# One decode step of grouped-query attention with a cached context and a dense ReLU layer: the closing products on one group of columns, and wo loaded in other pieces

## The chip, the cores and the metric

The kernel runs on one core of one Trainium2 chip. All arithmetic is in 32-bit floats. The time is the device time of one execution in microseconds (us), the median of several runs. Beside the runs there is one profiled execution, with a record of every instruction on TensorE (PE for products, PEld for the loads of their weights), VectorE (DVE), ScalarE (ACT), GpSimd (POOL), of the DMA queues, and of the clock that TensorE was granted.

## The reference

One token x of 512 values is normalized. Its attention goes over 65536 cached keys and values, 32 query heads sharing 8 key and value heads; beside it runs a layer with 1792 hidden values; both results are added to x.

```python
x = A_x
xn = _layernorm(x, axis=-1)
return x + _A_ref(xn, A_k_cache, A_v_cache, A_wq, A_wo) + _B_ref(xn, B_w1, B_w2)

# _A_ref: D = 512, Hq, Hkv, Sk, Dh = 32, 8, 65536, 128
q = (x @ wq).reshape(B, Sq, Hq, Dh).transpose(0, 2, 1, 3)
scores = jnp.einsum("bhqd,bhkd->bhqk", q, k) * (Dh ** -0.5)
o = jnp.einsum("bhqk,bhkd->bhqd", _softmax(scores, axis=-1), v)
return o.transpose(0, 2, 1, 3).reshape(B, Sq, Hq * Dh) @ wo
# _B_ref: Dff = 1792
return jnp.einsum("bsf,fd->bsd", jnp.maximum(jnp.einsum("bsd,df->bsf", x, w1), 0), w2)
```

## The kernel before, in words

Two large buffers in the on-chip memory hold what is streamed in: `ks` for keys, later for w1 and w2, and `vs` for wq, then for values, later for wo. All large loads are issued by SyncE (SP) on one queue, in program order.

**Start.** x is normalized and q = xn @ wq is made from 32 slices of wq (line 279).

**Attention.** 8 heads with 4 steps each, 32 steps in all. A step multiplies one load of keys with the queries (line 343), takes the maximum and the exponentials, and multiplies the values with the weights so made (line 359, accumulated in `acc_o`). SP refills `ks` or `vs` as soon as the step that read it lets go of it.

**End.** After the last keys SP loads w1 and w2 into `ks`, and after the last values wo into `vs`, as 32 slices of 512 columns (`load_slices`, which issues one DMA for each entry of `WO` and keeps a mark for each slice: the semaphore of the DMA that brings it). PE then works in this order:

1. h = relu(xn @ w1): 16 products (line 442), then the heads' results are put together and divided (lines 452 to 493). The outcome is `hT`, the weights for the products with w2, and `sw`, those for the products with wo.
2. Four small products that add x to `acc_y` (line 513).
3. 14 products with w2 (`FB` = 14), written by `gather`, line 504. Each multiplies a column of 128 weights with a slice of 128 x 512 and adds the row of 512 that comes out to `acc_z`. In the records each such product is two weight loads and two matmul instructions.
4. 28 products with the first slices of wo (`DIRECT` = 28), the same `gather`.
5. DVE copies `acc_z` to `rows` (line 535) as soon as slice 27 is done.
6. Slices 28 and 29 of wo go straight to `acc_y` as four products of 128 columns each (line 539). Then come four products that sum `rows` over its 128 partitions into `acc_y` (line 524), and slices 30 and 31.
7. DVE transposes `acc_y` to `yt` (line 551), and SP writes y out.

The kernel addresses TensorE's columns of weights in four groups: a product whose output starts at row 0, 32, 64 or 96 of the accumulator stands on column group 0, 1, 2 or 3. `gather(c, ...)` writes row 32c of `acc_z` and so stands on group c; the calls give it `j % CT` with `CT` = 4, so that the products take the four groups by turns. The rows of `acc_z` that no product writes were set to zero at the start; the sum over all partitions in step 6 adds up whichever rows were used.

Between the products nothing sets the order but the order of the program and the marks: the first w2 product waits for `hT` and for w2, the first wo product for `sw` and its piece of wo, and a later one for its own piece.

Of the kernel before, what the change touches and what calls it, by code (L numbers as in the profile page):

```python
# [16 lines left out]
D = 512  # L17
# [4 lines left out]
CT = 4  # L22
# [12 lines left out]
R = HKV  # L35
SLICES = R * G
WQ = [4, 28]
WO = [16, 8, 4, 2, 1, 1]
DIRECT = 28
EPS = 1e-5  # L40

# [27 lines left out]
def attention_and_mlp_kernel(  # L69
# [32 lines left out]
    def place(name, *shape, rows=P):  # L102
        return nc.alloc_sbuf_tensor(name, [rows, *shape], F32).ap()
# [36 lines left out]
    total, oT, hT = place("total", HQ), place("oT", HQ), place("hT", 4 * CT)  # L140
# [11 lines left out]
    def load(engine, name, dst, src, n=16):  # L152
        sem = nc.alloc_semaphore(name)
        engine.dma_start(dst, src).then_inc(sem, n)
        return sem, n


    def load_slices(name, src, counts):
        marks = []
        for n in counts:  # L160
            cut = slice(len(marks) * D, (len(marks) + n) * D)
            marks += [load(sy, f"{name}{len(marks)}", vs[:, cut], src[:, cut])] * n
        return marks
# [152 lines left out]
    t1, t2 = ks[:, : A * DFF], ks[:, A * DFF : A * DFF + FB * D]  # L316
    w1_in = load(sy, "w1_in", t1, w1.rearrange("p a f -> p (a f)"))
    w2_in = load(sy, "w2_in", t2, w2.rearrange("p j n -> p (j n)"))
    sy.wait_ge(v_free, 1)
    wo_in = load_slices("wo", wo.rearrange("h (i r) g f -> (h i) (r g f)", r=R), WO)  # L320

# [47 lines left out]
    with nc.Fori(0, HKV, engines=[ENG.DVE], head_slot={ENG.DVE: 110}):  # L369
# [36 lines left out]
        last = bias[:, NP - 1, :G].unsqueeze(1).to_broadcast([P, NP - 1, G])  # L406
# [56 lines left out]
    for j in range(2):  # L463
# [4 lines left out]
    hT_in = DV.op(lambda e: e.tensor_copy(hT.rearrange("p (c j) -> p c j", c=CT), hid), hid_in)  # L468
# [23 lines left out]
    sw_in = DV.op(  # L492
        lambda e: e.reduce_sum(
            sw.rearrange("p (r g) -> p r g", r=R), spread.rearrange("p r h g -> p r g h"), axis=AX.X
        ),
        DV.mark,
    )
# [3 lines left out]
    def gather(c, lhsT, row, marks, last=False):  # L501

        PE.op(
            lambda e: e.matmul(acc_z[32 * c : 32 * c + 1, :], lhsT, row, start=c not in begun, stop=last),  # L504
            *marks,
        )
        begun.add(c)
# [6 lines left out]
            x4_in,  # L514
        )
    for j in range(FB):
        gather(j % CT, hT[:, j : j + 1], t2[:, j * D : (j + 1) * D], [hT_in, w2_in])

    for j in range(SLICES):
        if j == SLICES - 2:  # L520

            for c in range(CT):
                PE.op(
                    lambda e: e.matmul(  # L524
                        acc_y[32 * c : 32 * c + 1, :P], ones[:, 0:1], rows[:, c * P : (c + 1) * P],
                        start=False, stop=False,
                    ),
                    folded,
                )
        row = vs[:, j * D : (j + 1) * D]  # L530
        lhsT = sw[:, j : j + 1]
        if j < DIRECT:
            gather(j % CT, lhsT, row, [sw_in, wo_in[j]], last=(j >= DIRECT - CT))
            if j == DIRECT - 1:
                folded = DV.op(lambda e: e.tensor_copy(rows, acc_z), PE.mark)  # L535
        else:
            for c in range(CT):
                PE.op(
                    lambda e: e.matmul(  # L539
                        acc_y[32 * c : 32 * c + 1, :P], lhsT, row[:, c * P : (c + 1) * P],  # L540
                        start=False, stop=(j == SLICES - 1),
                    ),
                    sw_in, wo_in[j],
                )
# [47 lines left out]
```

## Time and profile before

| | |
|---|---|
| time, median of 3 runs | 1303.25 us (1303.14 to 1303.85) |
| span of the profiled execution | 1303.1 us |
| PE busy with products | 666.8 us (51%) |
| PE loading weights | 187.1 us (14%) |
| DVE / ACT / POOL busy | 268.4 / 76.0 / 4.1 us |
| DMA queue of SP, share of 16 engines | 99.6% |
| read from the memory outside the core | 560.99 MB, 431 GB/s over the span |

The span runs from the first to the last instruction of the profiled execution; it lies 0.15 us under the median of the runs. Busy time of an engine is the union of its instructions. A row of the timeline gives the start, the length, the engine, the line, the output and the inputs, the shape, and how many instructions were merged into the row; in brackets stands how long the engine was idle before it and what ended that.

### The profile page before, as it was taken

The page shows a single profiled execution, that of the slowest core. Times are in us where ns is not written, and L with a number is a line of the kernel's source. Part 1 is how long each engine was busy: PE and PEld are TensorE (multiplying, and loading weights), DVE is VectorE, ACT ScalarE, POOL GpSimd, SP SyncE. Part 2 cuts the span into 40 slices and gives each one's busy share as a digit, 9 for nine tenths or more (in the row PEclk, how much of TensorE's full clock was granted, in tenths as well). Part 3 has the DMA queues.
Part 4 walks back from the last instruction along what each step waited for, and adds up shares of the span by engine and source line. Part 5 has one row for each costly group of instructions (what it writes and reads, how often), then busy time and mean ns, then how long its engine had stood idle before and what let it go on. Part 6 is the DMA issues. An engine that isn't in the chain of part 4 may idle for free. (4 is left out here: it accounts for less than half of the span.)

```text
span 1303.1 us, 10664 instructions
## 1 busy us (share of the span) xinstructions
PE 666.8 (51%) x4512; PEld 187.1 (14%) x4512; DVE 268.4 (21%) x398; ACT 76.0 (6%) x292; POOL 4.1 (0%) x22
## 2 busy tenths in 40 slices
PE   3355456455446545545545545544544644553657
PEld 1111111111111111111111111111111111111111
DVE  2221122221112222012222112222112222211222
ACT  0000000000000000000000000000000000000000
POOL 0000000000000000000000000000000000000000
PEclk9676676777677677667677677767767766767768
DMA  9999999999999999999999999999999999999998
GB/s 419 419 418 449 420 449 420 449 420 449 420 449 420 449 420 435 435 422 445 420 449 420 449 420 449 420 449 420 449 420 439 431 422 445 420 449 420 449 418 359
DMA packets 10957, 561.06 MB, mean 431 GB/s; under 512 B 1476, under 2 KB 1480, under 8 KB 1864
## 3 DMA queue, kind: packets, MB, share of 16 engines
q1 hardware_dynamic: 10800, 561.00, 99.6%
q8 instruction: 3, 0.05, 0.0%
q10 hardware_dynamic: 152, 0.00, 0.0%
q14 instruction: 2, 0.02, 0.0%
HBM read 560.99 MB, written 0.00 MB: 431 GB/s over the span
## 5 line engine op out<-in xcount | busy, mean ns | idle before, releaser
L359 PE MATMUL acc_o<-vs,wt 128*16 128x512 f32 x2048 | 298.5, 748 | 176.0 <-PEq L355 176.0
L343 PE MATMUL pa<-ks,qcur 128*32 128x512 f32 x1024 | 177.1, 824 | 321.6 <-PEq L338 321.6
L375 DVE STREAM_TRANSPOSE tr<-pa 128x1024 f32<-128x1024 f32 x64 | 80.0, 1250 | 411.1 <-PE pa L343 411.1
L343 PE MATMUL pb<-ks,qcur 128*32 128x512 f32 x1024 | 141.6, 673 | 0.0
L421 ACT ACTIVATE wt<-tr,bias 128x128 f32<-128x128 f32 x128 | 64.3, 511 | 1085.3 <-ACTq L419 1085.3
L359 PEld LDWEIGHTS acc_o<-vs,wt 128*16 128x16 f32 x2048 | 70.0, 114 | 377.7 <-issue 377.7
L343 PEld LDWEIGHTS pa<-ks,qcur 128*32 128x32 f32 x1024 | 39.0, 134 | 429.7 <-issue 421.7
L375 DVE STREAM_TRANSPOSE tr<-pb 128x1024 f32<-128x1024 f32 x64 | 80.0, 1250 | 51.5 <-PE pb L343 51.5
L401 DVE SCALAR_TENSOR_TENSOR acc<-acc,alpha,acc_o 128x512 f32<-128x512 f32 x24 | 18.0, 748 | 352.2 <-PE acc_o L359 352.2
L343 PEld LDWEIGHTS pb<-ks,qcur 128*32 128x32 f32 x1024 | 42.5, 133 | 108.8 <-issue 89.7
L348 PE MATMUL pm<-ident,m 128*4 128x128 f32 x32 | 10.4, 326 | 87.7 <-DVE m L387 67.2
L399 DVE COPY acc<-acc_o 128x512 f32<-128x512 f32 x8 | 5.5, 691 | 121.5 <-PE acc_o L359 121.5
L349 PE MATMUL pm<-dg,ones 4*128 4x4 f32 x64 | 15.8, 315 | 21.4 <-DVE dg L391 21.4
L384 DVE TENSOR_REDUCE mc<-tr 128x4 f32<-128x512 f32 x24 | 24.1, 1006 | 1.8
L421 ACT ACTIVATION_READ_ACCUMULATOR wt<-tr,bias 128x1 f32 x128 | 23.9, 187 | 0.0
L348 PEld LDWEIGHTS pm<-ident,m 128*4 128x4 f32 x32 | 2.6, 81 | 116.8 <-DVE m L387 89.0
L349 PEld LDWEIGHTS pm<-dg,ones 4*128 4x128 f32 x64 | 13.0, 252 | 29.2 <-DVE dg L391 29.2
L350 PE MATMUL pm<-dg,rowg 4*128 4x1 f32 x64 | 15.1, 302 | 0.0
L279 PE MATMUL pa<-vs,tr 128*8 128x512 f32 x64 | 9.9, 772 | 8.6 <-DMA vs<-wq 7.3
L350 PEld LDWEIGHTS pm<-dg,rowg 4*128 4x128 f32 x64 | 13.9, 266 | 0.0
L504 PE MATMUL acc_z<-vs,sw 128*1 128x512 f32 x56 | 9.1, 817 | 6.2 <-DMA vs<-wo 6.2
L389 DVE TENSOR_REDUCE mg<-pm 4x1 f32<-4x128 f32 x32 | 8.9, 279 | 13.4 <-PE pm L348 13.4
(98 smaller groups left out, 94.6 us busy)
## 6 DMA issues: line engine op xcount, KB each, us to landing
vs<-wq SPq DMA_DIRECT2D x1, 7168.0 KB, 21.2
ks<-w SPq DMA_DIRECT2D x2, 3584.0 KB, 22.5
vs<-wo SPq DMA_DIRECT2D x1, 4096.0 KB, 16.9
vs<-wo SPq DMA_DIRECT2D x1, 2048.0 KB, 21.5
vs<-wq SPq DMA_DIRECT2D x1, 1024.0 KB, 4.6
vs<-wo SPq DMA_DIRECT2D x1, 1024.0 KB, 23.5
ks<-k SPq DMA_DIRECT2D x32, 28.8
vs<-v SPq DMA_DIRECT2D x32, 28.9
```

What stands on the lines that cost most here:

```text
L279: lambda e: e.matmul(pr[32 * c : 32 * c + HKV, :], xs[:, i, :], vs[:, i * 512 : (i + 1) * 512], start=(i < CT), stop=(i >= SLICES - CT),),
L343: i = te.matmul(tile_of[32 * c : 32 * c + 32, :], qcur, ks[:, at : at + TW], start=True, stop=True)
L348: te.transpose(pm[:G, :P], m, ident)._wait_ge(s_dve, 3).then_inc(s_max, 1)
L349: te.matmul(pm[:, P : P + G], ones[:G, :], dg[:, :G], start=True, stop=True)._wait_ge(s_dve, 4)
L350: te.matmul(pm[:, P + G : P + G + 1], rowg, dg[:, G : G + 1], start=True, stop=True).then_inc(s_max, 1)
L359: mm = te.matmul(acc_o[32 * c : 32 * c + WIDE * G, :], wt[:, i * WIDE : (i + 1) * WIDE, :].rearrange("p b g -> p (b g)"), vs[:, i * 512 : ...
L375: i = ve.transpose(tr[:, s * SUB : (s + 2) * SUB, :].rearrange("p b i -> p (b i)"), (pa, pb)[s // 2 % 2].rearrange("p i k -> p (i k)"),)._ ...
L384: i = ve.reduce_max(top, tr[:, :, :G].rearrange("p b g -> p g b"), axis=AX.X)
L389: ve.reduce_max(mg, pm[:G, :P], axis=AX.X)._wait_ge(s_max, 1)
L401: ve.scalar_tensor_tensor(flat, flat, alpha[:, n : n + 1], acc_o, op0=ALU.mult, op1=ALU.add)
L421: i = se.activation(wt[:, :, g], tr[:, :, g], AF.Exp, bias=bias[:, n, g : g + 1], scale=scale, accum_out=part[:, n, g : g + 1],)
L504: lambda e: e.matmul(acc_z[32 * c : 32 * c + 1, :], lhsT, row, start=c not in begun, stop=last),
```

## The change

The products with w2 and those with the first 24 slices of wo all stand on column group 0. Slices 24 to 27 of wo go on by turns over the four groups. wo comes in seven DMAs of 8, 8, 8, 4, 2, 1 and 1 slices; it was six, of 16, 8, 4, 2, 1 and 1.

```diff
-WO = [16, 8, 4, 2, 1, 1]
+WO = [8, 8, 8, 4, 2, 1, 1]
+SINGLE = 24
 DIRECT = 28
...
     for j in range(FB):
-        gather(j % CT, hT[:, j : j + 1], t2[:, j * D : (j + 1) * D], [hT_in, w2_in])
+        gather(0, hT[:, j : j + 1], t2[:, j * D : (j + 1) * D], [hT_in, w2_in])
...
         if j < DIRECT:
-            gather(j % CT, lhsT, row, [sw_in, wo_in[j]], last=(j >= DIRECT - CT))
+            gather(0 if j < SINGLE else j % CT, lhsT, row, [sw_in, wo_in[j]], last=(j >= DIRECT - CT))
```

On SP the loads at the program's end stood as follows before (`ks<-w` is w1 and w2; a slice of wo has 512 columns, so 128x8192 is a piece of 16 slices):

```order
L154 DMA ks<-w 128x7168 [waits k_free]
L154 DMA ks<-w 128x7168
L154 DMA vs<-wo 128x8192 [waits v_free]
L154 DMA vs<-wo 128x4096
L154 DMA vs<-wo 128x2048
L154 DMA vs<-wo 128x1024
L154 DMA vs<-wo 128x512 x2
```

And with the change:

```order
L155 DMA ks<-w 128x7168 [waits k_free]
L155 DMA ks<-w 128x7168
L155 DMA vs<-wo 128x4096 [waits v_free]
L155 DMA vs<-wo 128x4096 x2
L155 DMA vs<-wo 128x2048
L155 DMA vs<-wo 128x1024
L155 DMA vs<-wo 128x512 x2
```

The piece of 16 became two pieces of 8; everything else on SP keeps its place.

On PE the products and their order stay the same, 14 with w2 and 28 with wo. Their waits before, from the first w2 product on (`wo16` is the semaphore of the piece that begins with slice 16; the semaphore of the first row is one of the framework's that was used again, and carries w2's landing):

```order
L504 MATMUL acc_z<-ks,hT 1x512 [waits Activation_sequencer_49]
L504 MATMUL acc_z<-ks,hT 1x512 x13
L504 MATMUL acc_z<-vs,sw 1x512 [waits wo0,dve]
L504 MATMUL acc_z<-vs,sw 1x512 x15
L504 MATMUL acc_z<-vs,sw 1x512 [waits wo16]
L504 MATMUL acc_z<-vs,sw 1x512 x7
L504 MATMUL acc_z<-vs,sw 1x512 [waits wo24]
L504 MATMUL acc_z<-vs,sw 1x512 x3
L539 MATMUL acc_y<-vs,sw 1x128 [waits wo28]
```

And with the change:

```order
L505 MATMUL acc_z<-ks,hT 1x512 [waits Activation_sequencer_49]
L505 MATMUL acc_z<-ks,hT 1x512 x13
L505 MATMUL acc_z<-vs,sw 1x512 [waits wo0,dve]
L505 MATMUL acc_z<-vs,sw 1x512 x7
L505 MATMUL acc_z<-vs,sw 1x512 [waits wo8]
L505 MATMUL acc_z<-vs,sw 1x512 x7
L505 MATMUL acc_z<-vs,sw 1x512 [waits wo16]
L505 MATMUL acc_z<-vs,sw 1x512 x7
L505 MATMUL acc_z<-vs,sw 1x512 [waits wo24]
L505 MATMUL acc_z<-vs,sw 1x512 x3
L540 MATMUL acc_y<-vs,sw 1x128 [waits wo28]
```

One wait is new, before slice 8. The rows don't show the column group; it is in the address of the output alone.

## The prediction

> **What bounds the kernel now.** I read the page's table of slices first, then the chain that ended last, then the timeline of the last 25 us.
>
> ```profile
> PE   3355456455446545545545545544544644553657
> DMA  9999999999999999999999999999999999999998
> DMA vs<-wo 1%; PE acc_o L359 1%; PE acc_z L504 1%; DVE rows L535 0%; PE acc_y L539 0%; DVE yt L551 0%; PE acc_y L524 0%; DVEq L397 0%
> ```
>
> The DMA engines are busy in every slice while PE is busy half the time: the 32 steps of attention are bound by the loads, and nothing that the change touches lies there. What counts is the end, where the chain in order of time shows who comes last:
>
> ```profile
> 1273.14 16.94 DMA vs<-wo
> 1290.08 0.14 issue
> 1290.22 9.20 PE acc_z L504 x56
> 1299.41 0.02 issue
> 1299.44 0.70 DVE rows L535
> 1300.14 0.04 issue
> 1300.18 0.40 PE acc_y L524 x8
> 1300.58 0.56 PE acc_y L539 x16
> 1301.14 0.02 issue
> 1301.17 0.41 DVE yt L551
> ```
>
> The first piece of wo lands at 1290.08, PE multiplies for 9.2 us, DVE copies `acc_z`, and a tail follows. From the copy's start to the span's end are 1303.1 - 1299.44 = 3.66 us. PE's own timeline around it:
>
> ```profile
> 1279.16 0.70 PE L484 MATMUL pb<-tr,octet 128*128 128x256 f32 x2 [0.74 <-DVE tr L478]
> 1279.79 0.39 PE L513 MATMUL acc_y<-x,ones 1*1 1x128 f32 x8
> 1280.41 3.60 PE L504 MATMUL acc_z<-ks,hT 128*1 128x512 f32 x28 [0.23 <-DMA ks<-w]
> 1290.22 9.06 PE L504 MATMUL acc_z<-vs,sw 128*1 128x512 f32 x56 [6.21 <-DMA vs<-wo]
> ```
>
> The w2 products start at 1280.41, when w2 lands (0.23 us of idle that a DMA ended), and are done at 1284.01. Then PE is idle for 6.21 us until wo. So before, this stretch has slack, and a slower PE first eats that slack.
>
> **What one product costs on one group.** A product is two matmul instructions. How many run at a time? The durations, by line:
>
> ```profile
> L504 PE MATMUL acc_z<-ks,hT x28: 590/592/593, 1280.4 to 1283.4; 128*1 128x512 f32 x28
> L452 PE MATMUL pb<-fins,selg x8: 378/379/381, 1276.5 to 1276.7; 128*4 128x256 f32 x8
> ```
>
> 256 columns more take 592 - 379 = 213 ns, so 0.83 ns a column; 512 columns occupy their group for 0.426 us, and the other 0.166 us of the 592 ns is a latency. 28 instructions of 0.426 us are 11.9 us of streaming, done in 3.60 us: several run at once. The weight loads show how many. This is PEld where the clock is full, in the q products (the same 512 columns, four groups by turns), first and last row of seven equal steps:
>
> ```profile
> 26.59 0.10 PEld L279 LDWEIGHTS pa<-vs,tr 128*8 128x8 f32 x4 [0.42 <-issue]
> ...
> 29.59 0.10 PEld L279 LDWEIGHTS pa<-vs,tr 128*8 128x8 f32 x4 [0.33 <-issue]
> ```
>
> Four loads every (29.59 - 26.59)/7 = 0.4286 us, which is the time one instruction of 512 columns occupies its group. Four groups, one instruction in each: the turns give a factor of four. On one group a product then takes 2 x 0.4286 = 0.857 us, where four products now share that time.
>
> Do two successive instructions overlap in the same columns? The row of line 484 at 1279.16 above answers: two instructions on all 128 columns, 256 columns long, together 0.70 us, with these durations:
>
> ```profile
> L484 PE MATMUL pb<-tr,octet x2: 379/431/483, 1279.2 to 1279.5; 128*128 128x256 f32 x2
> ```
>
> The second starts 0.70 - 0.379 = 0.32 us after the first; the first is 0.483 - 0.379 = 0.10 us longer since it waited for its own weights; so the second streams 0.22 us behind it, the price of 256 columns (0.213 us). In the same columns they queue, they don't overlap. [...]
>
> Does the weight load of the next instruction add to it? It lasts 79 to 84 ns, and the first row of the w2 products has eight loads at once, two for each of four groups, while the first four matmuls had only begun:
>
> ```profile
> 1280.41 0.11 PEld L504 LDWEIGHTS acc_z<-ks,hT 128*1 128x1 f32 x8 [0.52 <-DMA ks<-w]
> L504 PEld LDWEIGHTS acc_z<-ks,hT x28: 79/83/84, 1280.4 to 1283.0; 128*1 128x1 f32 x28
> ```
>
> So a group takes its next weights while it streams, and the load is hidden. Bounds: 0 and 83 ns an instruction; I take 0.
>
> **The clock.** At half clock the steps of four are twice as long:
>
> ```profile
> 1291.03 0.15 PEld L504 LDWEIGHTS acc_z<-vs,sw 128*1 128x1 f32 x4 [0.70 <-issue]
> ...
> 1295.29 0.15 PEld L504 LDWEIGHTS acc_z<-vs,sw 128*1 128x1 f32 x4 [0.70 <-issue]
> ```
>
> (1295.29 - 1291.03)/5 = 0.852 us. Which clock will the new stretch have? The windows below are cut at instants at which the clock can change (all its changes in this trace lie whole multiples of 3.41 us apart); columns are length, PE busy with its instructions, granted clock, DMA share and GB/s.
>
> ```profile
> 961.55:964.97 3.42, 1.36 (x16) 1.00 0.84 364
> 964.97:968.38 3.41, 0.00 (x0) 0.50 0.75 327
> 1282.41:1285.82 3.41, 1.60 (x12) 1.00 1.00 432
> 1285.82:1289.23 3.41, 0.00 (x0) 1.00 0.83 356
> ```
>
> The first window, busy 1.36 us with 16 instructions, was followed by half clock; the third, busy 1.60 us with only 12 instructions of the same 512 columns (the last four of w2 run two at a time, on two groups), was followed by full clock. Fewer instructions over more time kept the clock: it goes by the time in which anything streams, not by how many groups do. With the change PE streams without a gap from 1280.41 on, starts at full clock, and I expect full clock to the end. The half clock that the wo products meet now, after their idle window, goes away; that relief is within the sum.
>
> **The sum**, on the profiled execution's own time:
>
> - Start: 1280.41, set by w2's landing; the loads up to there are unchanged.
> - Group 0 takes 14 + 24 products and slice 24, 39 x 2 = 78 instructions. The last starts 77 x 0.4286 = 33.00 us after the first, at 1313.41, and ends 0.592 us later at 1314.00. Slices 25 to 27 stand on the other groups beside slice 24, and cost nothing more.
> - Before, these products ended at 1290.22 + 9.06 = 1299.28, and the copy came 0.16 us later. The delay is 1314.00 - 1299.28 = 14.72 us.
> - The tail of 3.66 us keeps its length: no DMA wait stands in it after the copy. Span: 1314.00 + 0.16 + 3.66 = 1317.8 us; with the 0.15 us by which the median lies above the span, 1318.0 us.
>
> **The pieces of wo.** The issues and landings, medians from issue to landing:
>
> ```profile
> vs<-wo SPq DMA_DIRECT2D x1, 4096.0 KB, 16.9
> vs<-wo SPq DMA_DIRECT2D x1, 2048.0 KB, 21.5
> vs<-wo SPq DMA_DIRECT2D x2, 256.0 KB, 24.5
> 1273.14 3.52 SPq L154 DMA_DIRECT2D vs<-wo  x6
> ```
>
> One more DMA takes SP some 0.5 us more (six take 3.52 us), done about 1277, when the queue is still delivering w2: free. Slices 0 to 7 should land halfway between w2 and the old first piece, about 1280.4 + 9.7/2 = 1285.2, slices 8 to 15 at 1290.1, 16 to 23 about 1273.6 + 21.5 = 1295.1, the last about 1275.4 + 24.5 = 1299.9. Group 0 comes to slice 0 at 1280.41 + 28 x 0.4286 = 1292.41, to slice 8 at 1299.3, to slice 16 at 1306.1 and to slice 24 at 1313.0. Each finds its piece 7 us or more after landing: the finer pieces, which would let PE start 4.9 us sooner, are worth nothing here, the new wait costs nothing, and the bound at the end passes from the loads to PE. Without that cover the added DMA would cost at most its 0.5 us.
>
> **The rivals.**
>
> 1. *One group streams as fast as four* (the group in the address isn't what sets the pace, so that the change doesn't do what it says). For it: nothing but that no row here shows 512 columns on one group alone. Against it: the pair of line 484. Then the loads stay the bound, at the place of slices 24 to 27: these land about 1297.5 (their 512 KB between the pieces above), two starts and the latency later, at 1298.5, the copy's input is ready, 0.8 us earlier than now; but the last slice lands at 1299.9, and its products now begin at about 1300.6, so at most 0.7 us is won. Time 1302.6 to 1303.3, not slower. It decides once an instruction on one group takes less than (1298.7 - 1280.4)/77 = 0.24 us. Chance 3%.
> 2. *Partial overlap in one group*, by the middle of the two spacings the rows allow (0.107 and 0.4286): 0.27 us. 77 x 0.27 = 20.8, products end at 1301.8, span 1305.6, time 1305.8. Against it again line 484. Chance 2%. [...]
> 3. *The clock falls*, because one group of four counts as a quarter of the work. For it: a window of light work, 1.36 us, lost the clock. Against it: the windows above. It would fall after the first window that holds one group alone, at 1285.82, when (1285.82 - 1280.41)/0.4286 = 12.6 instructions have started; the other 64.4 at 0.852 us take 54.9, so the last starts at 1340.7, and the time is about 1345.5. A single window of half clock costs 3.41/2 = 1.7 us. Chance 4%.
> 4. *The weight loads show*, 83 ns for each of 77 steps: 6.4 us more, 1324.4. Against it: the eight loads at 1280.41. Chance 3%.
>
> **How the numbers follow.** The forecast, queueing at full clock, has 88%; its own range is 1317 to 1319 (the runs before spread over 0.7 us, w2's landing moves with them, and the step of 0.4286 us is known to 0.001 us, 0.1 us over 77). The range of 1316.5 to 1321.0 takes in one window at half clock (1319.7) and a part of the weight loads. What it leaves out is rivals 1 to 4, 12%, and a rest of the forecast. 0.2%, 2.6 us, is about what a measurement can tell from no change. Rival 1 and half of rival 2 make "same", 4%; a gain over 2.6 us would need work to leave the loads before the end, and none does: 1%. Slower: 95%.
>
> **What the changed profile would show.** The w2 products as one row from about 1280.4, some 12.2 us long, with weight loads one every 0.43 us instead of four; wo's products straight behind them with no wait for a DMA, until about 1314.0; granted clock 1.00 from 1280 to the copy; DMA done by about 1300, idle at the span's end; the tail unchanged at 3.66 us. A spacing near 0.51 us would point to rival 4, 0.85 us to rival 3, below 0.43 us to rivals 1 and 2. The forecast is wrong if the wo products wait for a piece, or if the last of them ends outside 1313 to 1316.

## The result, and the profile after

The changed kernel takes 1319.49 us (median of 4 runs, 1318.6 to 1320.35), the kernel before on the same chip 1303.2 us: a ratio of 1.0124, 95% interval 1.0109 to 1.0138. It is 16.3 us slower; 1318.0 was predicted, in a range of 1316.5 to 1321.0.

The four runs fall into two pairs, 1318.6 and 1318.7, 1320.29 and 1320.35. The profiled execution of the changed kernel belongs to the first: its span is 1317.4 us, its time 1318.7. The experiments below take up the second pair.

The page of the changed kernel, the lines that answer to those shown of before:

```profile
PE   3345445445545544554554454465455446445569
DMA  9999999999999999999999999999999999999994
PE acc_z L505 3%; DMA ks<-w 2%; PE pa L344 0%; PE pb L344 0%; DVE rows L536 0%; PE acc_y L540 0%; DVE yt L552 0%; PE acc_y L525 0%; SPq L155 0%; DVEq L375 0%
```

In the last slice PE and DMA have changed places: PE is at 9, DMA at 4. In the chain, the landing of wo (1% before) is gone; it goes from the landing of w2 straight through the products. Its end in order of time:

```profile
1252.89 27.02 DMA ks<-w
1279.91 0.04 issue
1279.96 32.89 PE acc_z L505 x83
1312.85 0.12 PE acc_y L540 x5
1312.97 0.03 issue
1313.00 0.73 PE acc_z L505
1313.73 0.02 issue
1313.76 0.70 DVE rows L536
1314.46 0.04 issue
1314.51 0.40 PE acc_y L525 x8
```

One piece of 33 us on PE stands where the wait for wo and 9.2 us of products were. The timeline shows its pace (weight loads, one for each matmul instruction):

```profile
1279.96 12.18 PE L505 MATMUL acc_z<-ks,hT 128*1 128x512 f32 x28 [0.50 <-DMA ks<-w]
1280.39 0.08 PEld L505 LDWEIGHTS acc_z<-ks,hT 128*1 128x1 f32 x1 [0.34 <-issue]
1280.82 0.08 PEld L505 LDWEIGHTS acc_z<-ks,hT 128*1 128x1 f32 x1 [0.34 <-issue]
...
1291.97 21.19 PE L505 MATMUL acc_z<-vs,sw 128*1 128x512 f32 x55
...
1312.58 0.39 PE L540 MATMUL acc_y<-vs,sw 128*1 128x128 f32 x6
1313.00 0.59 PE L505 MATMUL acc_z<-vs,sw 128*1 128x512 f32 x1
```

One weight load where four stood, every 0.43 us. From 1279.96 to the start of group 0's last instruction at 1313.00 there are 77 steps: 33.04/77 = 0.4291 us each. wo's products follow w2's without a wait for a DMA.

### The profile page after: what moved, and what is told of

Its sections match the earlier page's. It is cut to its first block, busy times and chain, and to the rows that moved or that the text cites. A ratio compares the mean times of both kernels' runs of the same rounds, so it can differ in the third digit from the quotient of the medians.

```text
span 1317.4 us, 10665 instructions
## 1 busy us (share of the span) xinstructions
PE 682.4 (52%) x4512; PEld 190.1 (14%) x4512; DVE 268.4 (20%) x398; ACT 76.0 (6%) x292; POOL 4.1 (0%) x22
## 5 line engine op out<-in xcount | busy, mean ns | idle before, releaser
L344 PE MATMUL pb<-ks,qcur 128*32 128x512 f32 x1024 | 138.7, 661 | 0.0
L505 PE MATMUL acc_z<-vs,sw 128*1 128x512 f32 x56 | 21.6, 592 | 0.0
L505 PE MATMUL acc_z<-ks,hT 128*1 128x512 f32 x28 | 12.2, 592 | 0.5 <-DMA ks<-w 0.5
```

The costliest lines, as they stand in the source:

```text
L344: i = te.matmul(tile_of[32 * c : 32 * c + 32, :], qcur, ks[:, at : at + TW], start=True, stop=True)
```

## The experiments

All changes are against the changed kernel. Times are medians; the kernel before ran beside each set (1303.54, 1303.34 and 1303.35 us in the three sets).

**The pieces of wo alone.** All products go by turns again.

```diff
-SINGLE = 24
+SINGLE = 0
...
-        gather(0, hT[:, j : j + 1], ...
+        gather(j % CT, hT[:, j : j + 1], ...
```

> Only wo's new pieces (8, 8, 8, 4, 2, 1, 1); all products by turns over four groups, as before. Theory (the loads bound this end, the groups bound the changed kernel): PE starts on wo about 5 us earlier, but the last slice still lands near 1299.9, so 1302.5 to 1303.5 us, no measurable difference from before. Rival (the pieces carry a part of the loss, by the seventh DMA or the new wait): 1304 us or more.

Measured: 1303.51 us, ratio 1.0002 (0.9993 to 1.0011). PE's timeline in this run:

```profile
1284.94 1.90 PE L505 MATMUL acc_z<-vs,sw 128*1 128x512 f32 x16 [1.33 <-DMA vs<-wo]
1289.73 3.29 PE L505 MATMUL acc_z<-vs,sw 128*1 128x512 f32 x16 [2.90 <-DMA vs<-wo]
1294.63 1.90 PE L505 MATMUL acc_z<-vs,sw 128*1 128x512 f32 x16 [1.60 <-DMA vs<-wo]
1297.13 1.04 PE L505 MATMUL acc_z<-vs,sw 128*1 128x512 f32 x8 [0.60 <-DMA vs<-wo]
```

PE starts on wo 5 us sooner, and then waits before every piece. (The second row is longer than the first since the clock was at half there: the granted clock is 0.50 from 1289.18 to 1292.60.) The pieces alone carry no part of the loss, and bring nothing that can be measured: the loads bound this end.

**The grouping alone**, with the old pieces.

```diff
-WO = [8, 8, 8, 4, 2, 1, 1]
+WO = [16, 8, 4, 2, 1, 1]
```

> Only the grouping, with the old pieces of wo (16, 8, 4, 2, 1, 1). Theory (group 0 is the queue, and comes to wo at about 1292, after the piece of 16 has landed near 1290): the time of the changed kernel, 1318.6 to 1320.4 us, with wo's products straight behind w2's. Rival (the pieces matter to the changed kernel): different by more than 1 us.

Measured: 1318.51 us, ratio 1.0115 (1.0099 to 1.013); of four runs three lay at 1318.45 to 1318.52 and one, the profiled one, at 1320.46. The whole loss is the grouping's: with the old pieces too, wo's products follow w2's without a wait.

```profile
1280.04 13.87 PE L505 MATMUL acc_z<-ks,hT 128*1 128x512 f32 x28 [1.03 <-DMA ks<-w]
1293.75 21.19 PE L505 MATMUL acc_z<-vs,sw 128*1 128x512 f32 x55
```

This profiled run is of the kind near 1320.3 us, and w2's products take 1.7 us longer in it (13.87 for 12.18). Windows laid on the grid of the clock's changes (in each of the traces of before and after they lie whole multiples of 3.413 us apart); length, PE busy with its instructions, granted clock, DMA share, GB/s; the last row is from the changed kernel's own profile, a run of the kind near 1318.6 us:

```profile
1276.77:1280.18 3.41, 1.64 (x14) 1.00 1.04 440
1280.18:1283.59 3.41, 3.41 (x5) 0.50 0.94 404
1283.59:1287.01 3.42, 3.42 (x9) 1.00 0.96 412
...
1277.72:1281.13 3.41, 2.19 (x13) 1.00 1.00 420
```

PE was busy for 1.64 us of the window in which it waited for w2; in the next, which begins 0.14 us after the queue, the clock was 0.50, and in the one after it 1.00 again. Half of 3.41 us is 1.7 us, the distance between the two kinds of runs. The two longer runs of the changed kernel weren't profiled; that they lost a window in the same way fits their times, and isn't shown.

**Only w2's products on one group**, the new pieces, wo by turns.

```diff
-SINGLE = 24
+SINGLE = 0
```

> New pieces; only the 14 w2 products stand on group 0, all wo products go by turns. Theory (only what pushes past the loads costs): w2 lasts 12.2 us instead of 3.6 and ends near 1292.4, in what was idle time; PE keeps full clock, 14 steps of 0.4286 us for wo end near 1298.6, under the last landings; 1302.5 to 1303.5 us, no measurable difference. Rival (each product on one group costs its 0.64 us wherever it stands): 14 x 0.64 = 9 us more, 1312 us.

Measured: 1303.82 us, ratio 1.0003 (0.9994 to 1.0012). The profile's chain ends

```profile
1252.88 26.89 DMA ks<-w
1279.77 0.04 issue
1279.81 18.34 PE acc_z L505 x84
1298.16 0.02 issue
1298.18 0.70 DVE rows L536
```

The copy that follows PE's 84 instructions starts at 1298.18; in the run with all products by turns it started at 1298.32. So 8.6 us more of w2's products (12.2 for 3.6) cost nothing measurable: they fill what was idle time, and wo's 14 steps then run without a gap. Now PE stands in the chain without slack. The runs spread more, 1303.09 to 1304.98, as they would if some of them lose a window of clock; that wasn't profiled.

**Only wo's products on one group**, the new pieces, w2 by turns.

```diff
-        gather(0, hT[:, j : j + 1], ...
+        gather(j % CT, hT[:, j : j + 1], ...
```

> New pieces; w2 by turns, the first 24 wo products on group 0. Theory: PE is free when slices 0 to 7 land at about 1285.2, at full clock, 48 steps of 0.4286 us to the last start at 1305.8, then 0.59 + 0.16 + 3.66: span 1310.2, time 1310 to 1312 us. Rival (losses add: the change cost 16.3 us for 38 products, 24 of them cost 24/38): 10.3 us, 1313.5 us or more; if w2's products were what cost, about 1303.

Measured: 1311.73 us, ratio 1.0062 (1.0048 to 1.0076), runs from 1311.44 to 1311.75.

```profile
1280.04 3.60 PE L505 MATMUL acc_z<-ks,hT 128*1 128x512 f32 x28 [0.50 <-DMA ks<-w]
1285.03 21.19 PE L505 MATMUL acc_z<-vs,sw 128*1 128x512 f32 x55 [1.39 <-DMA vs<-wo]
...
1306.05 0.59 PE L505 MATMUL acc_z<-vs,sw 128*1 128x512 f32 x1
```

The queue begins at 1285.03, when slices 0 to 7 land, and its last start is at 1306.05, 49 steps of 0.429 us later (one step more than the expectation counted). The losses don't add: w2's part costs 0 alone, wo's part 8.2, both 15 to 16, since w2's part eats the time that wo's part would have had, from 1285.0 to 1292.0.

**The same with the old pieces.**

```diff
-        gather(0, hT[:, j : j + 1], ...
+        gather(j % CT, hT[:, j : j + 1], ...
...
-WO = [8, 8, 8, 4, 2, 1, 1]
+WO = [16, 8, 4, 2, 1, 1]
```

> Old pieces of wo (16, 8, 4, 2, 1, 1); w2 by turns, the first 24 wo products on group 0. PE is idle from about 1283.6 until the piece of 16 lands near 1289.7, so the clock falls to a half. Theory (one group alone brings the clock back, as four did after 5.9 us): about 7 instructions at 0.852 us in the first 5.9 us, the other 41 steps at 0.429 us, last start near 1313.2, copy near 1313.9, span 1317.6, time 1317 to 1320 us, against 1311.7 with the finer pieces. Rival (one group counts as a quarter and the clock stays at a half): 48 x 0.852 = 40.9 us, 1335 us or more.

Measured: 1318.49 us, ratio 1.0114 (1.0097 to 1.0131). The windows of its profile, columns as above:

```profile
1285.04:1288.45 3.41, 0.00 (x0) 1.00 0.86 370
1288.45:1291.86 3.41, 2.28 (x3) 0.50 0.99 423
1291.86:1295.28 3.42, 3.42 (x5) 0.50 0.96 400
1295.28:1298.69 3.41, 3.41 (x9) 1.00 0.66 254
```

After the idle window (0.00 us busy) the clock was 0.50, and after one window that a single group filled (3.42 of 3.42 us busy) it was 1.00 again: 5 instructions in that window, 9 in the next of the same length. Here, where wo's products have the time to use it, the finer pieces are worth 6.8 us (1318.49 against 1311.73): the earlier start (1285.03 for 1289.58 in the profiles) and the clock that isn't lost (a row of 21.19 us for 24.00).

**Two groups by turns** for w2 and for wo's first 24.

```diff
-        gather(0, hT[:, j : j + 1], ...
+        gather(j % 2, hT[:, j : j + 1], ...
...
-            gather(0 if j < SINGLE else j % CT, ...
+            gather(j % 2 if j < SINGLE else j % CT, ...
```

> New pieces; the w2 products and the first 24 wo products by turns over groups 0 and 1 only. Theory (a group is a queue of its own, two give half the time of one): 0.429 us a product; w2 ends near 1286, each piece of 8 takes 3.4 us and is done before the next lands 4.9 us later; the loads bound the end again: 1303 to 1304.5 us. Rival (only all four groups together run side by side, or two share more than their columns): the time lies well between, 1308 us or more.

Measured: 1304.17 us, ratio 1.0006 (0.9996 to 1.0015).

```profile
1280.04 6.17 PE L505 MATMUL acc_z<-ks,hT 128*1 128x512 f32 x28 [0.64 <-DMA ks<-w]
1286.05 7.30 PE L505 MATMUL acc_z<-vs,sw 128*1 128x512 f32 x32
1294.64 4.03 PE L505 MATMUL acc_z<-vs,sw 128*1 128x512 f32 x22 [1.29 <-DMA vs<-wo]
```

w2's 14 products take 6.17 us, of which 0.17 are the latency: 0.429 us a product, half of one group's. The 16 of the second row come to 0.446 us each, in all 0.26 us above that pace; I put that down to a wait for the second piece, an estimate: eight products from 1286.05 on are done at 1289.48, and with all products by turns PE started on that piece at 1289.73. PE waits for wo again (1.29 us before the third row), and the loads bound the end. Two groups take half of the 0.858 us that a product takes on one, as two queues side by side would.

**More work in the wait for w2.** Four products that multiply w1 once more into a bank that nobody reads, ahead of w2's products.

```diff
+    for c in range(CT):
+        PE.op(
+            lambda e: e.matmul(pa[32 * c : 32 * c + 1, 1, :], ones[:, 0:1], w[:, 0, :512], start=True, stop=True)
+        )
     for j in range(FB):
```

> The changed kernel with four products more, by turns, that multiply w1 once more into a bank that nobody reads; they stand in the wait for w2, about 0.86 us of streaming, and may hold up w2's products by 0.3 us. Theory (the runs near 1320.3 are those in which the window before w2's products streamed less than about 0.36 of its 3.41 us, lost the clock and ran one window of 3.41 us at half clock, 1.7 us): with the filling all runs lie at 1318.4 to 1319.2 us, and the profile shows full clock from w2 to the end. Rival (the two kinds of runs come from the loads or from elsewhere): runs near 1320.3 to 1320.7 us remain.

Measured: 1319.08 us, ratio 1.0121 (1.0104 to 1.0138), runs from 1318.58 to 1319.47. The profile has a window at the same place as the one that lost the clock in the run of the grouping alone:

```profile
1276.73:1280.14 3.41, 2.61 (x23) 1.00 0.90 377
1280.14:1283.56 3.42, 3.42 (x9) 1.00 1.02 436
```

PE is busy for 2.61 us instead of 1.64, and the clock is 1.00 in the next window too. (The 0.36 in the expectation is an estimate from the traces; the last section has the windows behind it.) Two of the four runs lie above the 1319.2 us that was expected at most, and none near 1320.3. Once more, beside the changed kernel itself:

> The filled wait once more. Theory: no run above 1319.6 us, full clock from w2 to the end in the profile. Rival: some of the runs above 1320 us, as in three of eight runs of the kernels without the filling.

> The changed kernel itself once more, on the same chip as the filled wait. Theory (the clock lost ahead of w2 in some runs): again two kinds of runs, near 1318.6 and near 1320.3 us, or in the profile a full clock with span near 1317.3 or a window of half clock with span near 1319.0. Rival (loads or launch): a spread without a gap.

Measured: the filled wait 1319.46 us (1319.3 to 1319.64), just over the bound that was set for it, the changed kernel 1318.47 us (1318.3 to 1318.6), this time without a late run; its profile has a span of 1317.3 us, and rows of 12.18 us for w2's and 21.19 us for wo's products, the lengths of the changed kernel's first profile, where the clock was 1.00. So no run of the filled kernel is near 1320.3 in eight, against three in twelve of the kernels without it; that is too few to settle it by counting, but the windows show how the one profiled late run came about. The filling itself costs up to 1 us; in one of its two profiles PE comes to it late:

```profile
1279.74 1.04 PE L519 MATMUL pa<-ks,ones 128*1 128x512 f32 x8
1280.17 0.08 PEld L505 LDWEIGHTS acc_z<-ks,hT 128*1 128x1 f32 x1 [0.33 <-DMA ks<-w]
1280.60 0.59 PE L505 MATMUL acc_z<-ks,hT 128*1 128x512 f32 x1
```

Group 0 is still at the filling when w2 lands, and the queue begins at 1280.60 instead of 1279.96 as in the changed kernel's profile. It is no remedy.

**Less work in the wait for w2.** The four small products of x go behind w2's products.

> The changed kernel with the four small products of x (0.22 us of streaming) moved from before w2's products to behind them, so that the window before w2 is emptier; they then add 0.2 to 0.5 us to the queue. Theory (as for the filled wait): most runs lose the clock, 1320.4 to 1321 us. Rival (two kinds of runs from elsewhere): the same mix of two kinds as before, some 1.7 us apart, or one kind near 1318.9 us.

Measured: 1319.02 us, ratio 1.0128 (1.0111 to 1.0145); three runs at 1318.81 to 1319.09 and one at 1322.55. A miss: by their times three of the four runs kept the clock (the profiled one did: its rows of w2's and wo's products are 12.18 and 21.19 us long, and its queue is 0.42 us longer for the products of x within it), and the late one is 3.6 us late, not 1.7. That would fit two windows at half clock, but it wasn't the profiled one and stays open. What differs from run to run is not only where the clock's windows fall (the queue starts 2.24 us into its window in the changed kernel's first profile, and 3.27 us into it in the run that lost the clock), but also how long PE is idle until w2 lands: 1.03 us in the profiled run that lost the clock, 0.50 in the changed kernel's first profile, 0.35 in this one. By the count of the last section, and as an estimate from the rows of PE's timeline, a window of 3.41 us laid anywhere ahead of this queue streams for at least 0.49 of its length, and in the run that lost the clock for as little as 0.31. With the estimate of 0.36, then, no place of the windows would have lost the clock in this run, and 0.22 us less of streaming was not what decided.

## Why the prediction was right, point by point

- **The bound moves from the loads to PE**: shown. In the changed kernel the products follow w2's landing without a wait, and with the pieces alone or with two groups PE waits for wo again.
- **Four groups are four queues; on one group a product takes 2 x 0.4286 us**: shown: 0.4291 us a step over 77 steps on one group, and 0.429 us a product, half the time, on two; before, a step of four instructions on four groups took 0.4286 us. Rivals 1 and 2 (one group as fast as four, or partly overlapped) fall.
- **Weight loads hidden**: shown; the loads of L505 last 79 to 85 ns and the step is 0.4291 us, where one that held a load would be 0.51 us (rival 4).
- **The sum's term for the products**: 33.00 + 0.59 us predicted, 33.04 + 0.59 measured. The tail from the copy to the end: 3.66 predicted, 1317.4 - 1313.76 = 3.64 measured.
- **Start and offset: two terms that were off, in opposite directions.** The start at 1280.41 was 0.45 us late (1279.96 here). And the 0.15 us between span and time was wrong: in 41 later runs of the kernel before, the span is 1301.7 to 1302.8 us and the time 1.25 to 1.44 above it. The profiled execution of before, with a span of 1303.1, is later than all of them, and by that offset would have taken some 1304.4 us, more than any of the three runs that its span was set against. With 1.3 for 0.15, and 1279.96 for 1280.41, the sum gives 1318.7, which is the first pair of runs. That the forecast of 1318.0 came within 0.7 us of that pair is in part luck: the start's error took back a part of the offset's.
- **"Full clock to the end"**: right for the queue in the changed kernel's two profiles (31.87 us busy at clock 1.00 in the first, rows of the same length in the second), but too much as a statement on all runs. I looked at the windows behind w2's products, not at the one before them, where PE waits for w2. The grouping alone lost the clock there in its profiled run (0.50 from 1280.18 to 1283.59). If the second pair of runs did too, that is why the median lies 0.8 us above the first pair; the median also lies outside the forecast's own range of 1317 to 1319, and inside the wider one only because that had room for one window at half clock. Rival 3 itself, that one group cannot hold the clock, falls: one group ran 31.87 us at clock 1.00, and with the old pieces of wo a window at 0.50 that one group filled was followed by 1.00.
- **The pieces are worth nothing, and the new wait costs nothing**: shown, both beside the grouping (1318.51 and 1318.47 us with old and new pieces) and without it (ratio 1.0002).

## What to carry to other kernels

Where an engine sits behind a transfer, look for the amount by which its work can grow before it, not the transfer, ends last: here w2's products could take 8.6 us more for nothing, and the same grouping on wo cost 8 us. Two such edits don't add when they share that slack. And set a sum against a span with the offset of the runs it is compared with, not with another execution's median.

## What the runs showed of the hardware that I had not expected

- In these traces matmul instructions of another column group started ahead of earlier ones of the program that stood behind others on their own group. In the last rows of the changed kernel's timeline above, six instructions of line 540 start at 1312.58, before the last one of line 505 at 1313.00, which comes first in the program; with only w2 on one group, three of wo's instructions start at 1290.97, while w2's last starts at 1291.40:

```profile
1290.97 0.60 PE L505 MATMUL acc_z<-vs,sw 128*1 128x512 f32 x3
1291.40 0.59 PE L505 MATMUL acc_z<-ks,hT 128*1 128x512 f32 x1
```

- A window of one group did for the clock what one of four did. With the old pieces and wo on one group, the window to 1295.28 (3.42 us busy, 5 instructions, clock 0.50) was followed by clock 1.00; before, with four groups by turns, the window from 1292.65 to 1296.06 (3.41 us busy, 20 instructions, clock 0.50) was too. What sorts the windows at full clock here is the time in which anything streams, that is, the time covered by instructions when the last 0.166 us of each, its latency, are left out. The windows with 1.36 us (before) and 1.64 us (grouping alone, in many short bursts) of busy PE lost the clock and come to 1.19 and 1.17 us by that count; the window of 1.60 us (before, a single burst) kept it and comes to 1.44.
- The same count over every window of the traces of before and after: of 332 windows at full clock, the fullest that was followed by half clock streamed for 0.358 of its length (before, from 1077.61) and the emptiest that was followed by full clock for 0.359 (before, from 1019.58). So 0.36 of 3.41 us, or 1.23 us, is an estimate from these two traces of what kept the clock. Of 420 windows at half clock, the fullest that stayed at half streamed for 0.751 (before, from 159.42) and the emptiest that was followed by full clock for 0.757 (after, from 236.65). No run was made to try either number.
